# Moving an elementwise product from VectorE to GpSimd in a fused Hyena block with its backward pass, with changes to loads and buffers

## The chip, the cores and the metric

The kernel runs on one core of one Trainium2 chip. The metric is the device time of one execution in microseconds (us). Most executions of a kernel agree within about one per cent. A run over 1.5% above the fastest of the same kernel is called slow; fast runs are compared with fast runs only, of the same rounds on the same chip. In the profile's lines PE is TensorE, PEld its loads of weights, DVE is VectorE, ACT is ScalarE, POOL is GpSimd and SP is SyncE; L199 is line 199 of the kernel's source, which differs by a line or two from version to version. It stands in the helper `tt`, so nearly all two-input instructions of VectorE bear it, and the names of the tiles tell them apart. The granted clock of TensorE is given as a share of full speed.

## The reference

One forward pass and the gradients with respect to nine inputs. Sequence 2048, channels D = 1024, hidden size F = 3584, all bf16:

```python
def _A_ref(q, k, v, shift_k, ssm_k, ssm_D):
    k_shift = sum(k_pad[:, t:t + S, :] * shift_k[:, ks - 1 - t] for t in range(ks))     # 4 taps
    kv = k_shift * v
    y = irfft(rfft(kv, 2S) * rfft(ssm_k, 2S))[:S]         # long convolution per channel
    y = y + kv * ssm_D
    return q * y

def _B_ref(x, w_gate, w_up, w_down):
    h = (x @ w_gate) * (x @ w_up)
    return h @ w_down

xn = layernorm(A_q)
out = A_q + _A_ref(xn, A_k, A_v, shift_k, ssm_k, ssm_D) * silu(_B_ref(xn, w_gate, w_up, w_down))
# ... cut: outputs are out and its vector-Jacobian product with grad_out
```

## The kernel before

In the forward part two things run beside each other. TensorE multiplies the normalised rows by slabs of w_gate and w_up; ScalarE takes the result from PSUM (gut), the product of gate and up gives h (hN), and TensorE transposes h (hT) for the backward part. Meanwhile VectorE does the convolution: the four taps, and the Fourier transform's additions and complex product, for which TensorE does the small DFT matmuls (psP, psS, psY). One unit of gate and up, four row blocks long:

```python
def gu_unit(sl, b0, n, w, tick):
    gut = fg.tile([P, 4, 2, SLW], BF16, name="gut")            # pool of 2 buffers
    hN = fg.tile([P, 4, SLW], BF16, name="hN")
    for i in range(n):
        # ... cut: 8 matmuls into psg
        nc.scalar.copy(out=gut[:, i]..., in_=ps[:])
        flush(3)              # runs transposes that were put off 3 row blocks ago
        tick()                # lets the convolution's generator emit its share
    sta(GUd[...], gut[:, 0:n])                                 # store, issued by ScalarE
    tt(hN[:, 0:n], gut[:, 0:n, 0], gut[:, 0:n, 1], MUL)        # VectorE
    st(Hd[sl][...], hN[:, 0:n])                                # store, issued by GpSimd
    def turn():
        # ... cut: 8 transposes of hN on TensorE into ps
        nc.scalar.copy(out=hT[:, :, 0:n], in_=ps[:, :, 0:n])
        st(HTd[...], hT...)                                    # store, issued by GpSimd
    defer(turn)
```

`st` and the loads `cld` of the convolution are issued by GpSimd, in its program order; `ld` is issued by SyncE. The complex product on VectorE, per channel group, is a run of instructions with two inputs in SBUF:

```python
tt(m1, a, b_re, MUL)
for k in range(2): tt(m2[:, :, k], a[:, :, k], b[:, :, 1 - k], MUL)
tt(n1, asrc, b1, MUL); tt(n2, asrc, b1[::-1], MUL)
tt(m1[..., dst], m1[..., dst], n1, ADD); tt(m2[..., dst], m2[..., dst], n2, ADD)
tt(o[:, :, 0], m1[:, :, 0], m1[:, :, 1], SUB); tt(o[:, :, 1], m2[:, :, 0], m2[:, :, 1], ADD)
```

## Time and profile before

| | before |
|---|---|
| time | 2076.62 us, median of 3 runs (2070.27 to 2078.22) |
| PE busy | 1974.6 us of a span of 2072.6 us |
| forward part, to the first matmul of psbm (h times w_down) | 572.1 us |
| the same for D's and the weights' gradients, to the first matmul of psx | from 776.9 to 1656.6 us |
| the last stage, the gradient of x | 416.0 us |

The busy time over the forward part and over its densest 300 us (after the length: PE, PEld, DVE, ACT, POOL with instruction counts; granted TensorE clock; DMA share; GB/s):

```profile
0.00:572.00 572.00, 530.26 (x3304) 293.67 (x3305) 510.70 (x748) 281.53 (x439) 137.48 (x217) 0.99 0.69 234
...
200.00:500.00 300.00, 288.49 (x1799) 162.26 (x1797) 292.51 (x383) 141.78 (x224) 69.07 (x105) 0.99 0.66 227
```

VectorE is busy 292.5 of these 300 us and TensorE 288.5, and GpSimd 69. Off-loading VectorE to GpSimd is the natural idea. The product hN in the view by tile (durations min/median/max in ns), and who waited for it:

```profile
L199 DVE TENSOR_TENSOR hN<-gut x60: 284/685/693, 17.1 to 570.9; 128x1024 bf16<-128x1024 bf16 x54, 128x256 bf16<-128x256 bf16 x4, 128x512 bf16<-128x512 bf16 x2
...
  PE tr L567: 15.5, 9
```

Sixty products at 0.685 us, 39 us in all with the few short ones; TensorE waits for them 15.5 us in nine places.

### The profile page before, as it was taken

To read this page: it belongs to the slowest core of one execution; us is meant where nothing else is said; L and a number is where in the kernel's file an instruction comes from. 1 tells how busy PE (TensorE), PEld (TensorE's weight loads), DVE (VectorE), ACT (ScalarE), POOL (GpSimd) and SP (SyncE) were. 2 spreads that over 40 slices of the span, in tenths; PEclk is the share of its full clock that TensorE was granted. 3 is DMA by queue.
4 is the path that set the end of the run, shared out by engine and by line. 5 is a ranking of instruction groups with operands and counts; after the bars stand their busy time and mean duration, and the time that the engine had idled before them with its cause. 6 is when DMAs were issued, how large, how long until landed. Compare 5 with 4: busy or idle time off the path is not lost.

```text
span 2072.6 us, 29102 instructions
## 1 busy us (share of the span) xinstructions
PE 1974.6 (95%) x11626; PEld 1060.4 (51%) x11626; DVE 1488.6 (72%) x2009; ACT 617.7 (30%) x966; POOL 342.9 (17%) x499
## 2 busy tenths in 40 slices
PE   6989999999999998999898999999989999999998
PEld 3445555555544446666565555565444444444443
DVE  8689999999745556887799999989488024444343
ACT  5644544444423332222222222222122201101112
POOL 3212212221112111000122112011111101110100
PEclk9999999999999999999999999999999999999999
DMA  8675776567597869666888888668974989393921
GB/s 286 221 261 202 241 246 241 198 220 264 184 329 253 278 238 291 215 201 183 265 260 244 238 243 259 202 228 235 188 228 155 230 198 226 98 203 98 232 73 56
DMA packets 454792, 451.30 MB, mean 218 GB/s; under 512 B 237072, under 2 KB 381240, under 8 KB 440192
## 3 DMA queue, kind: packets, MB, share of 16 engines
q1 hardware_dynamic: 310320, 186.94, 35.4%
q0 software_dynamic: 45200, 189.08, 26.6%
q10 hardware_dynamic: 99136, 73.42, 11.7%
q8 instruction: 91, 1.49, 0.3%
q14 instruction: 45, 0.37, 0.1%
HBM read 208.15 MB, written 194.02 MB: 194 GB/s over the span
## 4 chain that ended last, share of the span: by engine, by line
PE 56%; DVE 19%; issue 14%; DMA 8%; POOL 2%; ACT 1%; SPq 1%; ACTq 0%; POOLq 0%; DVEq 0%
PE psx L1213 17%; PE psb L1092 10%; PE psbm L954 8%; PE psb L1190 7%; DVE W L199 5%; PE psg L553 5%; DVE m L199 5%; PE psb L1073 4%; DVE HX L199 2%; DMA B<-KFd 2%; DVE U L199 1%; DMA KSLd<-in_A_k_dram 1%; DMA B<-HFd 1%; DVE KX L199 1%; PE psY L404 1%
## 5 line engine op out<-in xcount | busy, mean ns | idle before, releaser
L553 PE MATMUL psg<-wslab,U 128*128 128x512 bf16 x1792 | 414.9, 382 | 7.1 <-ACT U L529 5.0
L1092 PE MATMUL psb<-U,U 128*128 128x512 bf16 x1792 | 396.9, 380 | 7.1 <-ACT dht L1075 3.3
L1213 PE MATMUL psx<-U,dgut 128*128 128x512 bf16 x1536 | 335.7, 379 | 2.4 <-DVE dxn L199 2.4
L1213 PEld LDWEIGHTS <-dgut 128*128 128x128 bf16 x1792 | 174.0, 98 | 213.3 <-issue 6.0
L1092 PEld LDWEIGHTS <-U 128*128 128x128 bf16 x1792 | 175.3, 98 | 209.8 <-issue 10.4
L553 PEld LDWEIGHTS <-U 128*128 128x128 bf16 x1792 | 173.6, 99 | 192.1 <-issue 7.3
L1073 PE MATMUL psb<-wdt,U 128*128 128x256 bf16 x1792 | 206.3, 276 | 10.7 <-ACT dht L1075 9.5
L1190 PE MATMUL psb<-U,U 128*128 128x512 bf16 x896 | 201.2, 386 | 10.9 <-DMA U<-Hd 6.1
L555 ACT CAST gut<-psg 128x512 bf16<-128x512 f32 x224 | 131.0, 585 | 227.6 <-PE psg L553 215.7
L1073 PEld LDWEIGHTS <-U 128*128 128x128 bf16 x1792 | 176.9, 99 | 35.7 <-issue 11.3
L954 PE MATMUL psbm<-U,ht 128*128 128x512 bf16 x784 | 171.8, 379 | 0.3 <-DMA ht<-HTd 0.3
L1096 ACT CAST wb<-psb 128x512 bf16<-128x512 f32 x112 | 65.5, 585 | 319.3 <-PE psb L1092 224.2
L199 DVE TENSOR_TENSOR m<-A,B 128x1024 bf16<-128x1024 bf16 (+1 forms) x160 | 116.7, 792 | 47.8 <-DMA B<-KFd 32.2
L1190 PEld LDWEIGHTS <-U 128*128 128x128 bf16 x896 | 88.3, 99 | 117.2 <-issue 11.7
L199 DVE TENSOR_TENSOR W<-W 128x1024 f32<-128x1024 f32 (+1 forms) x144 | 146.0, 1032 | 2.7
L199 DVE TENSOR_TENSOR dka<-dkh,Wbc 128x1024 bf16<-128x1024 bf16 x16 | 11.1, 692 | 165.8 <-DMA dkh<-DKSHd 165.8
L954 PEld LDWEIGHTS <-ht 128*128 128x128 bf16 x784 | 76.0, 98 | 89.5 <-DMA ht<-HTd 0.8
L1236 ACT ACTIVATE dx_t<-dxn 128x1024 bf16<-128x1024 f32 (+1 forms) x17 | 17.1, 1007 | 341.6 <-DVE dxn L199 290.2
L1075 ACT CAST dht<-psb 128x512 bf16<-128x512 f32 x112 | 65.2, 587 | 154.9 <-PE psb L1073 102.4
L1192 ACT CAST wbs<-psb 128x512 bf16<-128x512 f32 x56 | 32.7, 585 | 176.1 <-PE psb L1190 140.5
L199 DVE TENSOR_TENSOR W<-W,psP 128x512 f32<-128x512 f32 x128 | 80.7, 681 | 5.8 <-ACT W L229 5.8
L199 DVE TENSOR_TENSOR U<-U,dht 128x2048 bf16<-128x2048 bf16 x56 | 69.1, 1233 | 21.4 <-ACT dht L1075 21.4
(233 smaller groups left out, 2362.2 us busy)
## 6 DMA issues: line engine op xcount, KB each, us to landing
U<-GUd SPq DMA_DIRECT2D x28, 1024.0 KB, 7.5
DGd<-U ACTq DMA_DIRECT2D x56, 512.0 KB, 4.9
GUd<-gut ACTq DMA_DIRECT2D x54, 512.0 KB, 4.6
A<-DYFd POOLq DMA_DIRECT2D x16, 1024.0 KB, 8.0
U<-Hd SPq DMA_DIRECT2D x15, 1024.0 KB, 6.1
out_dram<-wb ACTq DMA_DIRECT2D x224, 64.0 KB, 3.1
Hd<-hN POOLq DMA_DIRECT2D x54, 256.0 KB, 3.5
HTd<-hT POOLq DMA_DIRECT2D x54, 256.0 KB, 3.4
```

The lines of the kernel that those rows point to most:

```text
L199: V.tensor_tensor(o, a, b, op)
L404: nc.tensor.matmul(ps[:, i, :], TI[:, j, r, k, :], gseg(G, r, j, k), start=(n == 0), stop=(n == 3))
L553: gu_mm[0] = nc.tensor.matmul(ps[:], XNT[q][:, dc, qi * P:(qi + 1) * P], w[:, dc].rearrange("p a f -> p (a f)"), start=(dc == 0), stop=(dc ...
L555: nc.scalar.copy(out=gut[:, i].rearrange("p a f -> p (a f)"), in_=ps[:])
L954: nc.tensor.matmul(ps[:, dh * 512:(dh + 1) * 512], ht(fc)[:, i * P:(i + 1) * P], WD[fc // 4][:, fc % 4, dh * 512:(dh + 1) * 512], start=(f ...
L1073: nc.tensor.matmul(ps[:, x * SLW:(x + 1) * SLW], DBMT[2 * hf + g][:, dc, (b % 4) * P:(b % 4 + 1) * P], wdt[:, dc, :], start=(dc == 0), sto ...
L1075: nc.scalar.copy(out=dht[:, 2 * e:2 * e + 2].rearrange("p b f -> p (b f)"), in_=ps[:])
L1092: nc.tensor.matmul(ps[:], XN[b // 4][:, b % 4, dc * P:(dc + 1) * P], dgus[b // 8][:, b % 8].rearrange("p a f -> p (a f)"), start=(b == 0), ...
L1096: nc.scalar.copy(out=wb[:].rearrange("p a f -> p (a f)"), in_=ps[:])
L1190: nc.tensor.matmul(ps[:], h[:, b, f * P:(f + 1) * P], DBM[b // 4][:, b % 4, dh * 512:(dh + 1) * 512], start=(b == 0), stop=(b == NB - 1))
L1192: nc.scalar.copy(out=wbs[:, dh * 512:(dh + 1) * 512], in_=ps[:])
L1213: nc.tensor.matmul(ps[:, dh * 512:(dh + 1) * 512], t[n][:, f, i * P:(i + 1) * P], WGU[n][:, f, dh * 512:(dh + 1) * 512], start=(n == 0 and ...
```

## The change

Its intent: relieve VectorE in the forward part, load k and v earlier, keep the transposing loads of late weights from blocking SyncE's queue (one held it for 26.40 us), and start D's gradient without a wait. The core of the diff:

```diff
 # head
-    nc.vector.tensor_tensor(diag[:], ident_f[:, 0:64], ident_f[:, 64:128], ADD)    # now after layer norm
-        root = nc.scalar.activation(r0_, vpe, ACT.Sqrt)
+        with tc.issue_after(act_copy[0].ins) if ... else nullcontext():
+            root = nc.scalar.activation(r0_, vpe, ACT.Sqrt)
-            nc.any.tensor_copy(XNT[q][...], ps[:])
+            if i % 2 == 0: act_copy[0] = nc.scalar.copy(out=XNT[q][...], in_=ps[:])
+            else:          V.tensor_copy(XNT[q][...], ps[:])
 # product of gate and up
-        tt(hN[:, 0:n], gut[:, 0:n, 0], gut[:, 0:n, 1], MUL)
+        nc.gpsimd.tensor_tensor(hN[:, 0:n], gut[:, 0:n, 0], gut[:, 0:n, 1], MUL)
 # two buffers for k and v
-            v = U[4][:, 0:2048].rearrange("p (a x) -> p a x", a=8)
+            v = U[4][:, 2048 * c:2048 * c + 2048].rearrange("p (a x) -> p a x", a=8)
-            k = kst.tile([P, 2, 11, P], BF16, name="k")
+            k = kst.tile([P, 2, 11, P], BF16, name="k", bufs=2)
-                nx = 2 * dp + c + 1
+                nx = 2 * dp + c + 2
+        load_kv(0, 1)
 # D's gradient: kvx is loaded before dyx; the pump starts at 10 ticks
-        bpump((bcnt[0] - 8) / (BT - 8))
+        bpump((bcnt[0] - 10) / (BT - 10))
 # late weights paced by the stores
-        if k in (1, 2, 3, 4, 5):
-            load_wgu(...)
+        with tc.issue_after(wst.ins) if k > 0 else nullcontext():
+            if k in (1, 2, 3, 4, 5):
+                load_wgu(...)
             # ... the same for load_dgut
-            ld(o_dwd[f0:f0 + P, :], wbs)
+            wst = ld(o_dwd[f0:f0 + P, :], wbs)
```

More of the change, by code (lines that the diff above doesn't have):

```diff
@@ L1 @@
-from contextlib import ExitStack
+from contextlib import ExitStack, nullcontext
 import numpy as np
@@ L486, in ln_load @@
         ld(x4[:, 0:n, :], xq[:, c, r0:r0 + n, :])
-    tr_ln = [None]
+    tr_ln, act_copy = [None], [None]
     def layer_norm(b0, n, x4):
@@ L503, in layer_norm @@
         r0_ = small("r0_")
-        root = nc.scalar.activation(r0_, vpe, ACT.Sqrt)
+        with tc.issue_after(act_copy[0].ins) if act_copy[0] is not None else nullcontext():
+            root = nc.scalar.activation(r0_, vpe, ACT.Sqrt)
         mean_b = small("mean_b", BF16)
@@ L528, in layer_norm @@
                 tr_ln[0] = nc.tensor.transpose(ps[:, dc, :], x4[:, i, dc * P:(dc + 1) * P], ident[:])
-            nc.any.tensor_copy(XNT[q][:, :, qi * P:(qi + 1) * P], ps[:])
+            if i % 2 == 0:
+                act_copy[0] = nc.scalar.copy(out=XNT[q][:, :, qi * P:(qi + 1) * P], in_=ps[:])
+            else:
+                V.tensor_copy(XNT[q][:, :, qi * P:(qi + 1) * P], ps[:])
         return last, root, st(XNd[:, b0:b0 + n, :], x4[:, 0:n, :])
@@ L707, in build_kernel @@
                 build_tables(ps_st, tg, ang)
+    tt(diag[:], ident_f[:, 0:64], ident_f[:, 64:128], ADD)
     for p_ in (lnp, lns, tg, bsb):
@@ L775, in load @@
         def load(ds):
+            kv = cx.tile([P, NB, P], BF16, name="kvx")
+            cld(kv[:], KVd[ds])
             x = cx.tile([P, NB, P], BF16, name="dyx")
             cld(x[:], DYd[ds])
-            kv = cx.tile([P, NB, P], BF16, name="kvx")
-            cld(kv[:], KVd[ds])
             return x, kv
@@ L1164, in build_kernel @@
             hs[2] = load_h(2, HSL[2])
-        if k in (1, 2, 3, 4, 5):
-            load_wgu(k - 1, u8((7, 8, 9, 10, 2)[k - 1], a=4))
-        if k in (6, 7, 8, 9):
-            ts.append(load_dgut(0, k - 6))
+        with tc.issue_after(wst.ins) if k > 0 else nullcontext():
+            if k in (1, 2, 3, 4, 5):
+                load_wgu(k - 1, u8((7, 8, 9, 10, 2)[k - 1], a=4))
+            if k in (6, 7, 8, 9):
+                ts.append(load_dgut(0, k - 6))
         if k == 11:
```

## The prediction

> **What bounds the kernel now.** I read the page's totals first, then busy time in stretches of 25 us, then the list of waits, then the timeline at the gaps of TensorE (PE). Totals and, for 115 to 551 us (the stretch in which the forward convolution runs beside the gate/up matmuls), all instructions and then those touching the PSUM tile psP (columns after the length: PE, PEld, DVE, ACT, POOL; in the psP line PE, DVE; then granted clock, DMA share, GB/s):
> ```profile
> PE 1974.6 (95%) x11626; PEld 1060.4 (51%) x11626; DVE 1488.6 (72%) x2009; ACT 617.7 (30%) x966; POOL 342.9 (17%) x499
> ...
> 115.00:551.00 436.00, 421.77 (x2638) 238.82 (x2636) 421.89 (x563) 208.38 (x329) 96.81 (x148) 0.99 0.67 229
> ...
> 115.00:551.00 436.00, 38.60 (x256) 80.70 (x128) 0.99 0.67 229
> ```
> PE has only 98 us idle in the whole run (2072.6 - 1974.6), so no change that only fills gaps can win more than about 5%. From 115 to 551 us PE and DVE are both 97% busy: whatever is added to DVE there lengthens the kernel. The psP line matters below: 80.7 us of DVE's time there goes to instructions with one operand in PSUM.
>
> The gaps that the change addresses, in order of time:
> ```profile
> 8.73 1.91 POOL L163 TENSOR_TENSOR m<-f,tcol 128x1024 int32<-128x1024 int32 x1
> 9.51 1.22 DVE L123 TENSOR_TENSOR diag<-ident_f 128x64 f32<-128x64 f32 x1
> 11.27 0.20 ACT L504 ACTIVATE r__229<-vpe 128x1 f32<-128x1 bf16 x1 [5.14 <-DVE vpe L502]
> 11.38 0.99 ACT L529 COPY U<-tr 128x1024 bf16<-128x1024 bf16 x1
> 12.42 1.03 PE L553 MATMUL psg<-wslab,U 128*128 128x512 bf16 x2 [3.49 <-ACT U L529]
> ...
> 109.08 2.36 DVE L199 TENSOR_TENSOR U<-k,Wbc 128x2048 bf16<-128x2048 bf16 x2 [10.05 <-DMA k<-KSLd]
> 114.62 1.03 PE L567 MATMUL tr<-ident,hN 128*128 128x128 bf16 x8 [6.45 <-DVE hN L199]
> 115.45 3.33 PE L553 MATMUL psg<-wslab,U 128*128 128x512 bf16 x8
> ...
> 797.37 0.93 PE L790 MATMUL psY<-kvx,dyx 128*64 128x64 bf16 x32 [4.17 <-DMA kvx<-KVd]
> ...
> 1459.23 26.40 SPq L1149 DMA_TRANSPOSE U<-in_B_w_up_dram  x1
> 1467.00 0.53 POOL L65 DMA_DIRECT2D B<-KFd  x1 [6.24 <-PE psY L894]
> 1493.69 3.63 DVE L199 TENSOR_TENSOR m<-A,B 128x2048 bf16<-128x2048 bf16 x5 [27.50 <-DMA B<-KFd]
> 1496.05 5.92 PE L1190 MATMUL psb<-U,U 128*128 128x512 bf16 x16 [4.73 <-ACT wbs L1192]
> 1508.56 6.49 PE L1190 MATMUL psb<-U,U 128*128 128x512 bf16 x16 [6.14 <-DMA U<-Hd]
> ```
> The reader is to see three things. At the head, a copy from PSUM stands in ACT's queue behind the square root of the next block, which waited for DVE, where the tiny diag took 1.22 us. At 109 us DVE waits 10 us for k, the product hN is queued behind that on DVE, and PE waits 6.45 us for it; PE then runs eight matmuls in 3.33 us. At 1459 us the sync queue is held for 26.4 us by a transposing load of late weights; the loads of B and Hd and the stores of wbs sit behind it, DVE loses 27.5 us and PE twice some 5 us.
>
> [...]in the backward stage where GpSimd makes a copy (ho) while DVE works:
> ```profile
> 1430.88 6.00 DVE L243 SCALAR_TENSOR_TENSOR B<-W 128x512 bf16<-128x512 f32 x4
> 1431.66 4.05 POOL L898 COPY ho<-yl 128x2048 bf16<-128x2048 bf16 x1 [0.46 <-ACT yl L896]
> 1463.70 2.49 DVE L243 SCALAR_TENSOR_TENSOR B<-W 128x512 bf16<-128x512 f32 x4
> ```
> Four equal DVE instructions take 2.49 us undisturbed and 6.00 us beside the copy: 3.5 us lost to a copy of 3.7 us (its time at 1467 us with DVE idle). The diag above is the same: 64 columns, 1.22 us, ending when GpSimd's m ends at 10.64.
> [...]The trace has 1.91 us for m (1024 columns, two inputs). I take 2.0 us for hN; no bf16 case is in the trace.
> [...]8 matmuls in 3.33 us after the 6.45 us gap against 1.73 us (8 x 216 ns), and 16 in 5.92 and 6.49 us against 3.46 us.
>
> **The change part by part.**
> Head (diag later, PSUM copies split by hand between ACT and DVE, square root behind the copy). The copy at 11.38 can go when its transposes end (about 9.0), so PE's 3.49 us gap shrinks by up to 2.4 us; diag's 1.2 us lies in the same chain. LayerNorm on DVE still paces the rest. Estimate -2.5 us.
> Two buffers for k and v. The load of c=1 no longer waits for the compute of c=0. DVE's waits for k sum to 16.9 us, 10.05 of them at 109 us. On PE that place costs 6.45 + (3.33 - 1.73) + about 0.4 for slow transposes = 8.5 us. But the k of the next pair needs a DRAM copy of k (KSLd) that landed only at 101 us, and GpSimd's queue is in order, so it can block there with the product now behind it. I credit -5 us.
> Product hN on GpSimd. 44 products of 0.68 us (30.1 us) leave DVE in 115 to 551 us. [...]share 1 - 80.7/421.9 = 81%. Lost per product 0.95 x 2.0 x 0.81 = 1.54 us, net 1.54 - 0.68 = +0.86 us, times 44 = +38 us on an engine that is 97% busy. A few us fit into its 14 us of idle time: +35 us. What it frees for certain is PE's waits for DVE's hN, 15.5 us in 9 places; but 6.45 of these are counted under k, and the rest come back as waits for psP and HX when DVE is the slower engine.
> D's gradient: kv is loaded before dy, and the backward pump starts at 10 ticks instead of 8, which puts another group of 16 matmuls (3.46 us) ahead of the first use. kv no longer queues behind dy, which needs the last stores. The gap of 4.17 us goes, and some of the 0.81 and 1.59 us after it: -5 us.
> Late weights paced by the stores. One transposing load per slab instead of five in a row. PE's loss there is 4.73 + 6.14 idle and (5.92 - 3.46) + (6.49 - 3.46) = 5.5 of slow clock, 16.4 us in all. After 1515 us the DMA share is 0.71 and PE is full, so there is room, and the first of these weights is used at 1656 us, long after. I credit -14 us.
> Sum: -2.5 - 5 + 35 - 5 - 14 = +8.5 us.
>
> **The rivals.**
> First, the lock costs little: the products fall where DVE is at psP or idle, or a bf16 product takes nearer 1 us. Then DVE loses about 0.8 us each, no more than it gives up, PE's waits for hN vanish, and this part gives about -15 us: total -41 us, about 2035. For it: [...]the author of a tuned kernel would hardly keep a loss of 2%. Against it: all measured collisions cost DVE nearly the whole GpSimd instruction.
> Second, GpSimd becomes a wait of its own: it is in order and also issues the loads and stores, some of which wait for DVE (28.7 us for KX, 14.6 for HX). A product stuck behind one makes PE's transposes wait and drop to half clock: +55 instead of +35, total about +28, 2105.
> Third, the pacing only moves the congestion: DMA share in 1436 to 1515 us is over 1, and the 1 MB loads still meet those of A and B. Then -14 becomes -5.
> I weigh the product at +35 (0.6), -15 (0.25) and +55 (0.15): 21 - 4 + 8 = +25. With -26.5 of the other parts this is -1.5; with a little taken off for the third rival I put it at the time before.
>
> **Range and chances.** Predicted 2078 us (before: 2076.6). Where the gaps close and the lock is mild it is 2040; where DVE takes the full lock and GpSimd's queue adds waits it is 2112. Faster by over 2% means under 2035 and needs the first rival in full: 0.12. Slower by over 2% means over 2118 and needs the second and third together: 0.14. Within 2%: 0.74.
>
> **What would show it.** hN among GpSimd's groups at about 2.0 us; DVE's multiply and add groups m, W and HX with a longer mean than 0.685 and 1.27 us in 100 to 600 us while W with psP stays at 0.68; the end of the forward stage (psbm starts at 588 us now) later by some 25 us. If those means are unchanged and psbm starts earlier, the lock argument is wrong. k: no 10 us wait of DVE near 109 us; if GpSimd waits there for the KSLd copy instead, my discount was right. D: no wait of PE for kvx. Late weights: no DVE wait of 27 us for B, no PE wait at the first slabs of the w_down gradient; if they stay, the third rival holds. The last stage (from 1656 us to the end, 416 us) should keep its length.

The prediction's "lock" is the loss shown at the copy: four VectorE instructions took 6.00 us beside GpSimd's 4.05 us and 2.49 us without it. That a product would cost every instruction of VectorE as much, but for those at psP (the share of 81%), was my estimate; no trace of the kernel before shows it.

## The result

The changed kernel took 2178.27 us, median of 4 runs (2174.75 to 2182.55), against 2073.44 for the kernel before in the same rounds: ratio 1.0528, 95% interval 1.045 to 1.0607. Ratios here are the mean time of one kernel's fast runs over that of the other's fast runs of the same rounds, so not quite the ratio of the medians. The profiled runs are of the fast state. The prediction of 2078 (2040 to 2112) was wrong: the kernel is slower by over 5%.

Where the time went, by the starts of TensorE's groups of matmuls:

| stage | before | after |
|---|---|---|
| forward part, to the first psbm | 572.1 | 699.2 |
| psbm | 204.8 | 204.5 |
| D's and the weights' gradients | 879.7 | 863.6 |
| last stage | 416.0 | 413.5 |

The loss is 127 us in the forward part; the rest gives back 19. The same two stretches of the changed kernel:

```profile
0.00:699.00 699.00, 552.97 (x3244) 303.31 (x3305) 534.12 (x686) 283.50 (x441) 382.24 (x277) 0.91 0.56 192
...
200.00:500.00 300.00, 227.42 (x1344) 127.21 (x1367) 237.83 (x273) 108.26 (x171) 172.29 (x106) 0.89 0.53 179
```

Read two things. First, VectorE isn't the limit any more: it is busy only 237.8 of the 300 us. Second, TensorE is slowed in two ways: it is idle 699 - 553 = 146 us where it was idle 572 - 530 = 42, and the same matmuls take 23 us longer, for the granted clock in the 300 us is 0.89 instead of 0.99. The two make up the 127 us. (Some matmul records are missing from a trace, so its count is lower; the weight loads, x3305 both times, are complete and are the better measure of progress: in the densest 300 us 1367 instead of 1797 were done.)

What TensorE waits for is in the tile's view (the first line is the product, the second TensorE's waits for it: us in total, times) and in the list of waits (last column: the longest):

```profile
L562 POOL TENSOR_TENSOR hN<-gut x60: 659/2136/22911, 16.2 to 696.5; 128x1024 bf16<-128x1024 bf16 x54, 128x256 bf16<-128x256 bf16 x4, 128x512 bf16<-128x512 bf16 x2
...
  PE tr L570: 112.7, 12
```

```profile
PE tr L570 <- POOL hN L562: 112.7, 12, 22.8
...
DVE U L198 <- DMA KSHd<-U: 41.3, 3, 20.4
DVE W L198 <- ACT W L228: 41.1, 20, 7.8
```

A median of 2.14 us is what was expected, the maximum of 22.9 us is not. Eight products, one for each group of channels, take 11 to 23 us; the 52 others together take 107 us. The timeline at one of the eight, start and length in us:

```profile
306.65 3.02 DVE L198 TENSOR_TENSOR m<-KX,HX 128x2048 bf16<-128x2048 bf16 x4
...
307.62 12.39 POOL L562 TENSOR_TENSOR hN<-gut 128x1024 bf16<-128x1024 bf16 x1
...
309.59 1.29 DVE L198 TENSOR_TENSOR m<-m 128x1024 bf16<-128x1024 bf16 x2
310.80 1.29 DVE L198 TENSOR_TENSOR KX<-m 128x1024 bf16<-128x1024 bf16 x2
...
312.00 3.62 DVE L198 TENSOR_TENSOR m<-KX,HX 128x2048 bf16<-128x2048 bf16 x5
315.54 1.29 DVE L198 TENSOR_TENSOR m<-m 128x1024 bf16<-128x1024 bf16 x2
316.75 1.29 DVE L198 TENSOR_TENSOR KX<-m 128x1024 bf16<-128x1024 bf16 x2
318.07 6.29 DVE L198 TENSOR_TENSOR W<-KX 128x2048 f32<-128x2048 bf16 x2
320.07 1.03 PE L570 MATMUL tr<-ident,hN 128*128 128x128 bf16 x8 [8.34 <-POOL hN L562]
...
320.89 3.62 PE L556 MATMUL psg<-wslab,U 128*128 128x512 bf16 x8
```

The product starts while VectorE is in its complex product, a run of instructions with two SBUF inputs that follow each other without a pause (each group starts 0.08 to 0.09 us before the end of the one ahead) and keep their normal lengths (over the forward part m and KX from m take 680 ns, 685 in the kernel before). It ends 2 us after the run is over, in the first instruction (W from KX) that needs the result of the instruction right before it: KX ends at 318.04, W starts at 318.07. TensorE waits 8.34 us for hN and then does eight matmuls in 3.62 us, half speed (undisturbed, 8 x 216 ns = 1.73 us); the clock granted from 320.0 to 324.5 us was 0.50. The chain of waits through this place has one item on it:

```profile
306.21 0.72 POOL HTd L65
306.93 0.09 issue
307.02 0.02 POOLq L562
307.03 0.19 POOL HFd L65
307.23 0.39 issue
307.62 12.40 POOL hN L562
320.02 0.05 issue
320.07 1.03 PE tr L570 x8
```

### The profile page after: what moved, and what is told of

Same layout as the page of the kernel before. It is cut to its first block, busy times and chain, and to the rows that moved or that the text cites. A ratio compares the mean times of both kernels' runs of the same rounds, so it can differ in the third digit from the quotient of the medians.

```text
span 2180.8 us, 28879 instructions
## 1 busy us (share of the span) xinstructions
PE 1986.9 (91%) x11440; PEld 1068.8 (49%) x11626; DVE 1510.8 (69%) x1947; ACT 619.8 (28%) x968; POOL 586.3 (27%) x559
## 4 chain that ended last, share of the span: by engine, by line
PE 58%; DVE 14%; issue 11%; POOL 10%; DMA 6%; ACT 1%; SPq 0%; ACTq 0%; POOLq 0%; DVEq 0%
PE psx L1219 18%; PE psg L556 9%; PE psb L1196 9%; POOL hN L562 8%; PE psbm L959 8%; PE psb L1097 6%; DVE W L198 4%; DVE m L198 3%; PE psb L1078 3%; DVE U L198 2%; DMA KSLd<-in_A_k_dram 1%; DMA B<-HFd 1%; PE tr L570 1%; DVE A L198 1%; PE psP L215 1%
## 5 line engine op out<-in xcount | busy, mean ns | idle before, releaser
L556 PE MATMUL psg<-wslab,U 128*128 128x512 bf16 x1732 | 428.8, 396 | 8.0 <-ACT U L530 3.0
L562 POOL TENSOR_TENSOR hN<-gut 128x1024 bf16<-128x1024 bf16 (+2 forms) x60 | 243.8, 4064 | 47.0 <-ACT gut L558 43.8
L570 PE MATMUL tr<-ident,hN 128*128 128x128 bf16 x448 | 38.9, 233 | 115.1 <-POOL hN L562 112.7
L198 DVE TENSOR_TENSOR W<-W 128x1024 f32<-128x1024 f32 (+1 forms) x144 | 139.3, 985 | 2.8
```

The lines of the kernel that those rows point to most:

```text
L198: V.tensor_tensor(o, a, b, op)
L556: gu_mm[0] = nc.tensor.matmul(ps[:], XNT[q][:, dc, qi * P:(qi + 1) * P], w[:, dc].rearrange("p a f -> p (a f)"), start=(dc == 0), stop=(dc ...
L562: nc.gpsimd.tensor_tensor(hN[:, 0:n], gut[:, 0:n, 0], gut[:, 0:n, 1], MUL)
L570: nc.tensor.transpose(ps[:, a, i, :], hN[:, i, a * P:(a + 1) * P], ident[:])
```

## The experiments

First question: which part of the change costs? **e1_hn_dve** is the changed kernel with hN back on VectorE; **e2_hn_pool_only** the kernel before with hN on GpSimd and nothing else.

```diff
-        tt(hN[:, 0:n], gut[:, 0:n, 0], gut[:, 0:n, 1], MUL)
+        nc.gpsimd.tensor_tensor(hN[:, 0:n], gut[:, 0:n, 0], gut[:, 0:n, 1], MUL)      # e2; e1 is the reverse
```

> The changed kernel with the product hN back on DVE, everything else of the change kept. If the product on GpSimd is the whole loss, the forward stage (first psg to last psg, 557 us before, 685 us after) returns to about 550 us or less and the time falls to about 2045 us (before minus the 16 us of the backward stage, 2.5 of the last stage and a few at the head). If two buffers for k and v, the order at the head or the other parts carry some of the loss, the stage stays over 580 us and the time over 2080 us.

> The kernel before with only the product hN moved to GpSimd. If that one line is the loss: about 2073 + 110 to 130 = 2185 to 2205 us, eight products of over 10 us on GpSimd, one per channel group. If the loss needs the other parts (loads of k ahead in GpSimd's queue), it stays under 2130 us.

e1: 2069.33 us, ratio 0.9999 (0.9964 to 1.0034). e2: 2178.6 us, ratio 1.052 (1.0455 to 1.0585). The one line is the whole loss; the four other parts together are worth nothing that can be measured (the 2045 us that I expected of e1 did not come). In e2 TensorE waits 111.2 us for hN, the longest 22.8, as in the changed kernel.

Second question: what holds the eight products? The theory (starvation), which no trace so far shows, is that GpSimd gets in only when VectorE pauses. **e3_breaks** puts a one-column copy into the forward product at four places per channel group, each of the last column that the instruction before it wrote, with the aim that VectorE has to wait for its own result. **e5_free_copies** was meant as its control: the same 32 copies at the same places of the source, but of a column of a table that nothing has just written.

```diff
+            if not conj: V.tensor_copy(brk[:], m[:, 1, n - 1, 1, 255:256])      # e3
+            if not conj: V.tensor_copy(brk[:], Dbc[:, 0:1])                    # e5
             yield 5.6 / parts
```

> The changed kernel with 32 one-column DVE copies inside the forward complex product, each reading the last column that the DVE instruction before it wrote[...]. Starvation theory[...]: no product over about 6 us, PE's waits for hN fall from 113 us to under 30 us, the time falls to 2090 to 2120 us. Theory of the prediction (DVE loses what GpSimd holds): no gain, 2180 us or more, as more holds fall on DVE. If GpSimd's queue order is the cause: no change within 10 us.

> The changed kernel with the same 32 one-column copies on VectorE as in the run with breaks, at the same places in the forward product, but each copies a column of a table that nothing has just written[...]. Theory 1 (GpSimd gets in only while VectorE has to wait for its own last result): the copies let nobody in; the longest hN stays above 15 us, TensorE's waits for hN stay near 110 us, the time is 2175 to 2190. Theory 2 (any instruction of VectorE that reads one SBUF input instead of two lets GpSimd in): the same as with the dependent copies, longest hN below 9 us, waits near 25 us, time near 2130. Theory 3 (only the longer, busier VectorE matters): slower than the changed kernel, 2185 or more.

e3: 2130.14 us, ratio 1.0279 (1.0213 to 1.0345). e5: 2180.3 us, ratio 1.0548 (1.05 to 1.0595). The product in e3, in the view by tile:

```profile
L567 POOL TENSOR_TENSOR hN<-gut x60: 661/2208/7774, 16.3 to 640.2; 128x1024 bf16<-128x1024 bf16 x54, 128x256 bf16<-128x256 bf16 x4, 128x512 bf16<-128x512 bf16 x2
```

and in e5:

```profile
L567 POOL TENSOR_TENSOR hN<-gut x60: 659/2129/22917, 16.2 to 688.1; 128x1024 bf16<-128x1024 bf16 x54, 128x256 bf16<-128x256 bf16 x4, 128x512 bf16<-128x512 bf16 x2
```

The longest product falls from 22.9 to 7.8 us in e3 and not at all in e5; TensorE's waits for hN are 23.7 us against 110.8. But e5 is no control. The view of the copies, first of e3 (those at the other line run from 159.5 to 611.0 us), then of e5:

```profile
L304 DVE COPY brk<-m x16: 139/142/146, 154.6 to 606.7; 128x1 bf16<-128x1 bf16 x16
```

```profile
L304 DVE COPY brk<-Dbc x16: 148/156/158, 57.7 to 64.7; 128x1 bf16<-128x1 bf16 x16
L312 DVE COPY brk<-Dbc x16: 148/156/157, 57.9 to 64.9; 128x1 bf16<-128x1 bf16 x16
```

The copies of e5 depend on nothing before them, and all 32 ran near 60 us, long before the first forward product at 148 us. Within the products e5 is the changed kernel once more. So e3 shows that breaking up VectorE's run lets GpSimd in, but not what about the copies does it: that they depend on the result just before them, or that they read one input from SBUF instead of two (theory 2 of e5's expectation). One of the places in e3:

```profile
413.80 7.46 POOL L567 TENSOR_TENSOR hN<-gut 128x1024 bf16<-128x1024 bf16 x1 [0.33 <-ACT gut L563]
...
417.47 1.81 DVE L199 TENSOR_TENSOR m<-KX,HX 128x2048 bf16<-128x2048 bf16 x2
419.20 0.14 DVE L304 COPY brk<-m 128x1 bf16<-128x1 bf16 x1
419.27 3.13 DVE L199 TENSOR_TENSOR m<-KX,HX 128x1024 bf16<-128x1024 bf16 x2
```

GpSimd gets in at the copy: its product ends 2 us later, and VectorE's next instruction, the first of the two in the last line, takes 2.53 us instead of 0.68. Yet no pause is to be seen. Each of the 32 copies starts 73 to 79 ns before the end of the instruction ahead of it, as the others in the run do. And in e15 (below) a held product gets in where VectorE comes to instructions with one input in PSUM, again without a pause (W from psP starts at 271.02, HX ends at 271.09; the product ends at 273.08):

```profile
268.61 2.48 DVE L199 TENSOR_TENSOR HX<-W 128x512 bf16<-128x512 f32 x4
268.71 4.37 POOL L559 TENSOR_TENSOR hN<-gut 128x1024 bf16<-128x1024 bf16 x1 [1.58 <-ACT gut L555]
271.02 2.47 DVE L199 TENSOR_TENSOR W<-W,psP 128x512 f32<-128x512 f32 x4
```

A pause is the other way in: in the changed kernel all instructions of VectorE beside the eight held products have two inputs in SBUF, and seven of the eight get in at an instruction that starts 34 to 35 ns after the end of the one before it. So the theory was too narrow: in these traces either a short pause or an instruction with at most one input in SBUF goes with GpSimd getting in, and e3's copies are of the second kind. Whether their dependence on a result plays a part was not tested.

The loss fell only by half, a little short of the 2090 to 2120 us expected, and VectorE was busy 552 us in the forward part of e3 against 534 in the changed kernel: after 15 of the 32 copies its next instruction takes over 2.5 us instead of 0.68, 28 us in all. What TensorE's waits for hN lost (23.7 us against 112.7), VectorE paid in part.

Third question: can slack buy the loss back? If TensorE's waits for the held products are the loss, then a later turn and more buffers should hide a product of 23 us. **e4_late_turn** transposes 10 row blocks later with five buffers for hN; **e11_late_turn_gut** has three buffers each for hN and gut and turns 7 row blocks later; **e12_slack** four for hN, three for gut, one for hT and 10 row blocks; **e15_slack_q** is e12 with the stores of hT issued by ScalarE instead of GpSimd. All four are the kernel before with hN on GpSimd, which without slack takes 5.2% longer (e2).

```diff
-        gut = fg.tile([P, 4, 2, SLW], BF16, name="gut")
+        gut = fg.tile([P, 4, 2, SLW], BF16, name="gut", bufs=3)         # e11, e12, e15
-        hN = fg.tile([P, 4, SLW], BF16, name="hN")
+        hN = fg.tile([P, 4, SLW], BF16, name="hN", bufs=4)              # e4: 5, e11: 3
-            flush(3)
+            flush(10)                                                   # e11: 7
-            hT = fg.tile([P, 2, 4, P], BF16, name="hT")
+            hT = fg.tile([P, 2, 4, P], BF16, name="hT", bufs=1)         # e12, e15
-            st(HTd[...], hT...)
+            sta(HTd[...], hT...)                                        # e15
     # all: flush() before the two places that load what the last turns stored
```

> The kernel before with the product on GpSimd, and the transposes of hN asked of PE 10 steps after the product instead of 3 (five buffers for hN). If PE's waits for late products are what costs: PE's waits for hN fall to under 20 us and the time to 2080 to 2110 us although GpSimd's long products stay. If DVE's lost time is the cost: the same as the run without the delay, within 15 us.

> The kernel before with hN on GpSimd as in the late-turn run, but with three buffers for gate and up and three for hN, and the transposes of a row group done 7 ticks later. The late-turn run moved TensorE's wait from hN to the eviction of gate and up, which waited for GpSimd to give back their buffer. Theory 1 (a GpSimd product held up to 23 us needs slack on both sides of it): waits of TensorE for hN and for gut together fall from 75 us to below 30, time 2100 to 2125. Rival ([...]no slack helps): stays at 2140 or more.

> The kernel before with hN on GpSimd, four buffers for hN, three for gate and up, one for hT, and the transposes of a row group 10 ticks later (about 23 us of slack on the one side, 18 on the other). Theory 1 (TensorE's waits for held products are most of the loss): its waits for hN and for gut together below 30 us (the late-turn runs: 75 and 68), time 2095 to 2125. Rival (VectorE's own loss sets the time): the waits fall, but other waits of TensorE for VectorE's products take their place, and the time stays at 2140 or more.

> The run with slack (hN on GpSimd, four buffers for hN, three for gate and up, one for hT, transposes 10 ticks later) with the stores of hT issued by ScalarE instead of GpSimd, so that no transfer TensorE or ScalarE depends on stands behind a held product. Theory 1 (waits for held products, direct or through GpSimd's queue, are most of the loss): TensorE's waits for hN, hT and gut together fall from 105 us to below 30, time 2095 to 2125. Rival (VectorE's own loss sets the time): the waits fall, TensorE waits for VectorE's products and loads behind them instead, time 2140 or more.

| run | time, ratio | TensorE's larger waits for hN, gut and hT |
|---|---|---|
| e4 | 2152.27, 1.0379 (1.0317 to 1.0442) | hN 11.0 us, gut 63.9 us |
| e11 | 2152.91, 1.0408 (1.0345 to 1.0471) | hN 59.0 us, gut 8.8 us |
| e12 | 2178.53, 1.0551 (1.0504 to 1.0598) | gut 60.0 us, hT 37.6 us |
| e15 | 2150.89, 1.0405 (1.0369 to 1.0441) | hN 22.1 us, hT 13.8 us, gut 6.1 us |

Each of the first three only moved the wait, so they could not decide. e12 was to remove it and showed another way in which a held product is felt, in its timeline:

```profile
203.57 22.92 POOL L559 TENSOR_TENSOR hN<-gut 128x1024 bf16<-128x1024 bf16 x1
...
226.78 0.58 POOL L65 DMA_DIRECT2D Hd<-hN  x1 [0.30 <-POOL hN L559]
227.36 0.72 POOL L65 DMA_DIRECT2D HTd<-hT  x1
...
230.14 1.01 ACT L568 COPY hT<-tr 128x1024 bf16<-128x1024 bf16 x1 [15.29 <-DMA HTd<-hT]
231.05 1.08 ACT L555 CAST gut<-psg 128x512 bf16<-128x512 f32 x2
```

The store of hT stands in GpSimd's queue behind the held product, and the queue keeps its order: hT was written by 210.08, the store is issued at 227.36. ScalarE waits 15.29 us for that store before it may write hT again, and the evictions that TensorE needs stand behind ScalarE's copy. The single buffer for hT, which I had cut to make room, opened this way. e15 closes it. TensorE's waits for hN, gut and hT fall to 42 us, from 111 for hN alone in e2, and the time is still 4% over the kernel before: the expectation of 2095 to 2125 fell, the rival's 2140 or more holds. VectorE is busy 549 us in the forward part although 39 us of products left it, and the larger waits of TensorE are now for VectorE's results (26.9 us for W in front of psP, against 4.0 in the kernel before).

Fourth question: what does it cost when nobody waits for a GpSimd product at all? **e13_spare** leaves hN on VectorE and lets GpSimd multiply two halves of a tile that nothing else uses; what it may cost was estimated from the changed kernel, where VectorE lost some 60 us beside 60 products. It wasn't paced by anything and all its products ran in the first 212 us. **e16_spare_q** has the products paced: hN times hN into a spare tile, with four buffers for hN, and the stores of hT issued by ScalarE. **e17_store_q** is its control, with the moved stores alone. **e18_memset_q** occupies GpSimd for as long, but with memsets, which read nothing.

```diff
         st(Hd[sl][...], hN[:, 0:n])
+        nc.gpsimd.tensor_tensor(spare[:, 0, 0:n * SLW], spare[:, 0, 0:n * SLW], spare[:, 1, 0:n * SLW], MUL)  # e13
+        nc.gpsimd.tensor_tensor(spare[:, 0:n], hN[:, 0:n], hN[:, 0:n], MUL)                                  # e16
+        nc.gpsimd.memset(hN[:, 4:10], 1.0)          # e18, three times; hN is widened by these unused columns
-            st(HTd[...], hT...)
+            sta(HTd[...], hT...)                     # e16, e17, e18
```

> The kernel before, hN on VectorE, and after each store of hN GpSimd multiplies two halves of a tile that no other engine touches, the same 60 products of up to 128x1024. No engine waits for a GpSimd product; its queue's later transfers do. [...](it grew by 23 us though 37 us of hN left it, so about 60 us lost): VectorE's busy time in the forward part about 570 us instead of 511, TensorE waits longer for hN and for the forward product, time 2110 to 2130. If the loss is almost all in waits for GpSimd's products: 2075 to 2095.

> The kernel before with hN on VectorE, four buffers for hN, the stores of hT issued by ScalarE, and after each store of hN a GpSimd product of hN with itself into a spare tile, paced by hN; no engine waits for it within 37 us. VectorE has all its old work[...]. From the unpaced spare run (86 us of VectorE's time for 60 products, 1.43 us each) and from the changed kernel (about 60 us): VectorE's busy time in the forward part 560 to 580 instead of 511. If VectorE sets the forward part, it is 40 to 60 us longer, time 2105 to 2130; if TensorE's 530 us of work still cover it, below 2090.

> Control: the kernel before with the stores of hT issued by ScalarE instead of GpSimd, nothing else. 60 issues of about 0.33 us on an engine that is 28% busy: ratio 0.998 to 1.003 by either theory.

> The kernel before, stores of hT issued by ScalarE as in the control, and after each store of hN three GpSimd memsets of 128x1536 into columns of the same tile that nobody reads, about 1.35 us each by the 1.80 us that a memset of 128x2048 took, so some 4.05 us in all per row group, as the held products took on average (4.06 us): GpSimd is occupied for the same 240 us, but reads nothing from SBUF. Theory 1[...]: VectorE's busy time in the forward part stays at 505 to 520 us, ratio 0.998 to 1.006. Rival (the occupied queue costs, through late loads and stores): ratio 1.02 to 1.04 with VectorE waiting for k and for the stores of HX and KX.

| run | time, ratio | GpSimd's extra work | VectorE busy in the forward part | length of the forward part |
|---|---|---|---|---|
| e17 (control) | 2067.23, 0.9982 (0.9953 to 1.0012) | none | 510.3 | 572.4 |
| e13 | 2140.7, 1.0381 (1.0325 to 1.0436) | 133 us of products, unpaced | 597.0 | 643.9 |
| e16 | 2155.79, 1.0423 (1.0373 to 1.0473) | 253 us of products | 562.1 | 665.0 |
| e18 | 2104.09, 1.0166 (1.0081 to 1.0251) | 250 us of memsets | 532.3 | 609.7 |

In e16 no engine waits for a product, and it loses 4.2% nevertheless, more than the 2105 to 2130 that was expected; e13, too, came out above its 2110 to 2130, with 86 us more of VectorE's time. The mean of the memsets fits neither expectation (0.998 to 1.006, or 1.02 to 1.04; its interval reaches into the second, and the verdict is unclear), so their trace has to be read. The densest 300 us of the control, of e18 and of e16, one fence each:

```profile
200.00:500.00 300.00, 285.50 (x1760) 162.10 (x1790) 291.34 (x381) 141.56 (x224) 46.92 (x75) 0.99 0.66 226
```

```profile
200.00:500.00 300.00, 280.78 (x1680) 156.57 (x1711) 282.01 (x363) 136.35 (x216) 166.60 (x164) 0.98 0.65 227
```

```profile
200.00:500.00 300.00, 255.92 (x1501) 140.73 (x1527) 276.66 (x331) 121.39 (x191) 174.29 (x84) 0.95 0.56 192
```

GpSimd is busy to the same extent in e18 and e16 (167 and 174 us), but TensorE gets 1711 weight loads done in the one and 1527 in the other, against 1790 in the control. So of the progress lost by e16 in this stretch, 79 of 263 loads, three tenths, come with an occupied GpSimd of any kind (its queue also issues the loads and stores of the convolution), and the other seven tenths only with instructions that read SBUF. The split is rough. The memsets write the tile hN and so wait for its store and its transposes (32.8 us in all), which e16's products don't; and no memset takes more than 1.5 us, while the longest product of e16 holds the queue for 24.6 us. VectorE's groups point the same way: first e18, then e16 (mean ns is the number after the comma).

```profile
L199 DVE TENSOR_TENSOR W<-W,psP 128x512 f32<-128x512 f32 x128 | 79.7, 681 | 2.5 <-PE psP L216 2.5
L199 DVE TENSOR_TENSOR KX<-W 128x512 bf16<-128x512 f32 x64 | 39.9, 685 | 0.0
...
L199 DVE TENSOR_TENSOR U<-k,Wbc 128x2048 bf16<-128x2048 bf16 x32 | 38.7, 1223 | 21.0 <-DMA k<-KSLd 13.6 <-DMA KSHd<-U 6.9
```

```profile
L199 DVE TENSOR_TENSOR U<-k,Wbc 128x2048 bf16<-128x2048 bf16 x32 | 50.6, 1583 | 32.5 <-DMA k<-KSLd 28.4 <-DMA XNd<-U 3.2 <-DMA KSHd<-U 0.5
...
L199 DVE TENSOR_TENSOR KX<-W 128x512 bf16<-128x512 f32 x64 | 44.7, 756 | 0.0
L199 DVE TENSOR_TENSOR HX<-W 128x1024 bf16<-128x1024 f32 x32 | 39.8, 1298 | 33.1 <-DMA HFd<-HX 33.1
```

Beside memsets the instructions with two inputs have the lengths that they have in the kernel before (685 and 1223 ns), beside products they are longer (756 and 1583 ns). What the memsets do slow lies in layer norm, whose instructions have one tensor input: U from U and RSTD takes 1116 instead of 489 ns, twelve times, x from x and RSTD 1901 instead of 482, four times, two casts of 128x4 1.8 instead of 0.17 us, three times each. With the smaller ones that is some 28 us of instructions, enough for all that VectorE's busy time grew (22 us). It is also where e18 loses most: of the 190 weight loads that it is behind the control at 500 us, 96 are lost in the first 100 us, in which layer norm runs. The last fence also shows the queue's share in e16: VectorE waits 33.1 us for the store of HX and 28.4 us for k (none and 17.8 in the control), both issued by GpSimd behind its products.

Fifth question: are the other parts worth anything? Each was put alone into the kernel before: **e6_pace** (late weights), **e7_kv2** (two buffers for k and v), **e9_dy** (loads and start of D's gradient), **e10_head** (head). **e8_no_kv2** has head, D's gradient and pacing; **e14_pace_dy** has the two that alone lay lowest. The edits are the parts of the diff above.

> The kernel before with the late weights paced by the stores alone. My prediction gave this part -14 us (2073 to 2059). Rival: the run with hN back on VectorE showed the four other parts together at zero, so the pacing may be worth -10 with another part giving it back (then this run shows about 2062), or itself be worth nothing (2070 to 2075, with waits of TensorE for the transposed weights only moved to other places).

> The kernel before with two buffers for k and v alone. My prediction gave this part -5 us. The run with hN on VectorE has its forward part 7.4 us longer than before although the head begins 2.5 us sooner, and of the parts in it only these buffers and the head touch the forward part. Theory A: the two buffers cost, forward part +6 to +10 us, time +5 to +10. Theory B: the head's other order costs, then this run is 0 to -5.

> The changed kernel with hN on VectorE and one buffer for k and v: head, order of loads for D's gradient and pacing remain. If the two buffers cost 7 us (theory A): about 7 us below the kernel before, ratio 0.9965. If the head's other order costs (theory B): same as the kernel before, ratio 1.000 to 1.003.

> The kernel before with the other order of loads for D's gradient and its start at 10 ticks alone. My prediction gave this part -5 us. Theory A (its wait at the start of D was on the path): the wait of TensorE for kvx at the start of D falls from 4.2 us to below 1 and the time to about 2065 (ratio 0.998). Theory B (the wait is given back as waits on ScalarE and VectorE behind it, as the run with hN on VectorE shows at the same place): ratio 0.999 to 1.002.

> The kernel before with the head's part alone (copies of the transposed rows shared out between ScalarE and VectorE, the square root after the copy, the sum of the identity's halves late). My prediction gave -2.5 us. The runs with it begin the forward matmuls 2.4 us sooner but end the forward part later than before. Theory A: the gain stays, ratio 0.999. Theory B: DMA, VectorE and the first waits set the forward part from there, the gain is given back within it, ratio 1.000 to 1.001.

> The kernel before with the two parts that alone lay below it: paced weights (0.9967) and the order and start of the loads for D's gradient (0.9979, an interval that holds 1). If they add up: ratio 0.9945, about 2058 us. If both gain on the same waits in the backward part: 0.996 to 0.998.

| run | predicted for the part | ratio, 95% interval |
|---|---|---|
| e6 pacing | -14 us | 0.9967 (0.9949 to 0.9985) |
| e7 two buffers | -5 us | 1.0014 (0.9991 to 1.0037) |
| e9 D's gradient | -5 us | 0.9979 (0.9944 to 1.0015) |
| e10 head | -2.5 us | 1.0006 (0.9979 to 1.0034) |
| e8 head, D and pacing | | 0.9989 (0.9966 to 1.0012) |
| e14 pacing and D | | 0.9994 (0.9968 to 1.002) |

Only e6's interval leaves out 1; its mean is about 7 us below the kernel before. e8 and e14 contain the same pacing and show less, so even this gain is not firm. The -14 was read from one profile. Its two waits of TensorE do come back in others without pacing, and so does VectorE's wait for B; here e2:

```profile
PE psb L1190 <- DMA U<-Hd: 8.8, 1, 8.8
...
DVE m L199 <- DMA B<-KFd: 29.4, 3, 23.9
```

while e7, not paced either, has no such wait of TensorE and a shorter one of VectorE:

```profile
DVE m L199 <- DMA B<-KFd: 13.5, 3, 8.5
```

The stage is the gradient of w_down, from its first matmul to the first of psx. In the 13 profiles without pacing (the kernel before, e2, e4, e7, e9 to e13, e15 to e18) it takes 203.1 to 219.5 us, 210.9 on average, and is over 205 in nine; in the seven with pacing (the changed kernel, e1, e3, e5, e6, e8, e14) it takes 203.0 to 203.1 every time, and TensorE waits for nothing there. So the pacing does what it was meant to do, but is worth 7.9 us on average in this stage, and the profile from which I credited 14 was at the upper end of what the stage takes. Why e8 and e14 as wholes don't show it is open.

## Why the prediction was wrong, step by step

**The bound** was right as a description: TensorE and VectorE both near full in the forward part.

**The duration of the product** was right: 2.11 to 2.14 us where it runs undisturbed, against the 2.0 that I took.

**"Lost per product 0.95 x 2.0 x 0.81 = 1.54 us": this step failed**, in direction more than in size. It counts all of VectorE's instructions but those at psP as stopped. For those at psP that held (679 ns, 681 before), for the others only in part, as the sums below show. It has only VectorE stop for GpSimd, never GpSimd for VectorE. VectorE's busy time in the forward part went from 510.7 - 39.0 = 471.7 us of other work to 534.1, so 62.4 us lost, 1.04 us per product and not 1.54; net it is +23 us, less than the +38 predicted. Set against their medians in the kernel before, VectorE's instructions lose some 45 us beside 28 of the 52 short products, 1.6 us each, next to nothing beside the other 24, and 12.6 us at the ends of the eight long ones. In these eight it is first GpSimd that stops, for 11 to 23 us, while a run of VectorE's two-input instructions goes by (23 whole instructions beside the longest, of 22.9 us instead of 2.1; e3 shows it by breaking up the run; e5 shows nothing). I had the complex product's instructions in view and asked only what GpSimd does to them, not what they do to GpSimd.

**"44 = +38 us on an engine that is 97% busy ... +35 us"**: the forward part became 127 us longer, not 35. "What it frees for certain is PE's waits for DVE's hN, 15.5 us in 9 places" failed with it: they became 112.7 us in 12 places, for GpSimd's hN. A product that is held stops TensorE, whose transposes come a fixed three row blocks later, and TensorE comes back at half clock (3.62 us instead of 1.73 for eight matmuls, granted clock 0.50); the loads and stores in GpSimd's queue are held with it. That VectorE's added busy time translates one to one was the second mistake: in e16, with nobody waiting for a product, VectorE is busy 52 us more and the forward part is 93 us longer.

**"PE's waits for hN vanish"** (first rival) is refuted. **The second rival**, GpSimd as a wait of its own, was the right place with the wrong cause and size. It had a product stuck behind a transfer that waits for VectorE, worth +20 us with weight 0.15; it is the product itself that waits, and transfers are stuck behind it.

How far would a cure of the held products have gone? By e15 and e3 not to the end. Taking away nearly two thirds of the waits (e15), or four fifths with VectorE paying more (e3), leaves 4% and 2.8%. That the remaining part of e15 is VectorE's longer instructions and late transfers fits e16, but a split of the 127 us into VectorE's longer instructions, GpSimd's queue and TensorE's half clock to a few us was not reached, since each version that removes one bill adds to another.

**The four small parts**, predicted at -26.5 us, sum to nothing in e1. Head: the first gate/up matmul starts at 9.9 instead of 12.4 us, exactly the 2.5 predicted, and is given back within the forward part, which ends at 579.5 in e1. k and v: VectorE's waits for k fell only from 16.9 to 11.5 us in e1, and TensorE's wait for hN near 120 us is 9.9 us long there instead of 6.45; that k's copy in DRAM still has to land first, for which I had discounted, may be the reason, but was not tested. D: the wait for kvx went from 4.17 to 0.46 us for dyx, as predicted, without a difference in time that the runs can hold; part came back at once, as a wait for ScalarE of 3.15 us in e1 where it was 0.81. Pacing: the mechanism was right and the size about double (7.9 us on average in its stage, 7 in e6). The third rival's -5 was nearer in size, but not for its reason: the congestion did not stay.

**The signs that I named** hold in part. KX and HX rose from 685 to 809 and 788 ns in the changed kernel while W with psP stayed at 679; the wait for kvx is gone, that for B is 3.0 instead of 32.2 us, and the last stage kept its length. But m did not grow (680 ns, 685 before), which was the hint that there GpSimd is the one that waits; VectorE still waits for k, 8.8 us at once (11.5 in e1); and the forward part ends 127 us later, not some 25. One number in them was wrong from the start: psbm began at 572 us before, not 588.

## What to carry to other kernels

An engine with idle time is no free place for work that slows the busy one or is held by it: here GpSimd's products of 2.1 us rose to as much as 22.9 beside VectorE's two-input instructions, and KX and HX on VectorE rose from 685 to 809 and 788 ns. Ask of both engines who waits for whom, above all where one of them issues two-input instructions back to back, and whether a third engine waits for the loser. A product that takes 2 us by its median may have a maximum of 23, so read min, median and max, not the mean. Before crediting a wait seen in one profile, look how long it is in several executions of the same code. An instruction that is added as a control need not run where it is written: look for it in the trace.
